# A fused attention and expert kernel on one core: one weight load, one table step, sixteen filler products and one cast are placed elsewhere

## The chip, the cores and the metric

The kernel runs on one core of a Trainium2 chip. A core has a matmul engine (TensorE, PE in the profile, with its weight loads as PEld), three engines for elementwise work (VectorE or DVE, ScalarE or ACT, GpSimd or POOL), and SyncE (SP), which here only issues transfers. Each engine works through its own list of instructions in order and waits on semaphores for the others. Transfers between the device memory and the on-chip memory (SBUF) run on 16 DMA engines; they are issued from SP, from ACT or from POOL. Matmul results are written to PSUM, from where DVE or ACT must read them.

The metric is the time of one execution on the device in microseconds (us).

## The reference

Two steps follow each other. The first is attention over 8 batches of 8 heads, 576 positions and 64 values per head, where a position sees only positions of its own block of 64 and of earlier blocks:

```python
scores = scale * np.matmul(q, k.transpose(0, 1, 3, 2))
mask = block_i >= block_j                       # blocks of 64 positions
scores = np.where(mask, scores, -1000000000.0)
attn = softmax(scores)
x = np.matmul(attn, v)                          # then (8, 576, 512): heads side by side
```

The second sends every position through one of eight experts, and an expert may be carried over from the position before:

```python
logits = np.einsum('bsd,de->bse', x, w_gate)
local_gate = sigmoid(x @ w_local)
fresh_e = int(np.argmax(logits[b, s]))
e = fresh_e if s == 0 or local_gate[b, s] < 0.5 else prev_e
out[b, s] = softmax(logits[b, s])[e] * (np.maximum(x[b, s] @ w1[e], 0.0) @ w2[e])
```

All inputs and the output are float32. w1 is 8 x 512 x 1024 and w2 is 8 x 1024 x 512.

## The kernel before

**Attention.** A loop over `it` from -2 to 31 handles one pair of heads per round, as a pipeline: in one round the pair `a = it + 2` is turned (queries and keys are transposed on PE), the pair `c = it + 1` gets its scores, the pair `e = it` is multiplied with v, and the pair `x = it - 1` is normalised and written out as bf16 rows to a table `x_rows` in device memory. The order of the work is written by hand (`tc.manual_schedule`): each engine gets its instructions in the order in which the Python code emits them. SP issues the loads of q, k and v (`load_qk`, `load_ends`, `load_v`) and the stores of x (`rows_x`). In between POOL issues the loads of the expert weights, which are cast to bf16 on the way: `weights(n)` takes the next n of 64 portions ("quarters", one row block of a w1 or w2), and `load_weights`, line 63, issues them. All weights stay in two large tiles, `w1_bf` and `w2_bf`. The last two portions belong to w2 of the eighth expert; their place in `w2_bf` holds small tables of the routing until shortly before.

**Routing.** While attention runs, DVE works out which expert each position takes, in four groups of two batches: `gate`, `fresh`, `scan_rows`, `chosen`, `ranks`. From this come tables of which rows of `x_rows` belong to which tile of 128 positions of one expert (`toka` for the tiles whose positions are known after two groups, `tokb` after three, `tok2g` and `tok2s` after all), and the expert of each tile (`tea`, `teb`, `te2`). A dictionary `plan`, filled with `at(it, where, f)`, says in which round and at which place of the round each of these steps is emitted.

**Experts.** The last part is a loop over tiles `t`. For a tile, `gather(t)` (line 763, POOL) fetches 128 rows of `x_rows` by an indirect DMA; `turn_rows(t)` (line 784, SP) transposes them by a DMA; `first(t)` (line 779, DVE) copies the expert's w1 out of `w1_bf` into one of two fixed places, which the trace calls `natb` and `plb`; `up(t)` (line 798, PE, with the Relu on ACT at line 802) is the first product; `down(t)` (line 813, PE) is the second one, read straight from `w2_bf` at an offset known only at run time, so it has to wait for all loads into `w2_bf`; ACT scales its result (line 816) and POOL writes it out with `scatter` (line 822). PE's order around the start is `up(0)`, `up(1)`, the transposes of the last pair of heads (`results`, lines 673 and 679), `down(0)`, `up(2)`, the gate sums (`sums`, line 732), `down(1)`, `up(3)`, `down(2)`, `up(4)` and so on. Two dictionaries, `ahead` and `steps`, hang the remaining routing steps on these tiles: in every round first the entries of `ahead`, then those of `steps`. For `t = 1`, `ahead` holds `sums`: the gate sums of the last heads on PE, their addition and transposition on DVE (lines 744 and 749). `steps` holds `whole_b(NTB)`, `shares_a(2)` and `shares(2)`: eleven short DVE instructions of the tables (lines 328 to 334 and 280 to 287) that use nothing of those sums. After them `first(4)` stands in DVE's list.

**The start.** `load_qk(0)` loads the first pair in six transfers, over SP and ACT. Until they land, `warm(26)` gives PE 26 products of a tile of ones with itself (line 837), into a PSUM tile that is not read. `turns()` for the first pair transposes the keys (`w = 1`), then the queries (`w = 0`), four products each (line 974); `turned` then copies keys on ACT and queries on DVE, the latter as two casts of 256 columns (line 846). `tails()` transposes the last 64 positions (line 1013), and the products for the row maxima begin with `top(0, 2)` (line 558).

Of the kernel before, what the change touches and what calls it, by code (L numbers as in the profile page):

```python
# [16 lines left out]
def kernel(  # L17
# [11 lines left out]
    nc = tc.nc  # L29
# [107 lines left out]
    XGB, XBB = 3, 2  # L137
# [284 lines left out]
    def g_tile(n):  # L422
        return ps_gp.tile([P, 512], F32, tag=f"g{n}", name=f"g{n}")
# [3 lines left out]
    with tc.manual_schedule():  # L427
# [9 lines left out]
        def const(shape, dt, name):  # L437
            return cst.tile(shape, dt, tag=name, name=name)
# [11 lines left out]
        qh = const([P, S + 192], BF16, "qh")  # L450
# [132 lines left out]
        def rows(h):  # L583
            return slice(64 * h, 64 * h + 64)
# [169 lines left out]
        def table(t):  # L754
            return ((toka, toka, tea, t) if t < NTA else
                    (tokb, tokb, teb, t - NTA) if t < NT1 else (tok2g, tok2s, te2, t - NT1))

        def gather(t):
            g = table(t)
            n = 2 * GC * P if t < NTA else 3 * GC * P if t < NT1 else BS  # L760
            z = t % (2 * XGB)
            xg = ffn["xg", t] = scr[:, z * XW:z * XW + XW] if z < XGB else xgs[z - XGB]
            nc.gpsimd.indirect_dma_start(
                out=xg, out_offset=None, in_=x_dram[0:n],
                in_offset=bass.IndirectOffsetOnAxis(ap=g[0][:, g[3]:g[3] + 1], axis=0),
                bounds_check=n - 1, oob_is_err=False)
# [68 lines left out]
        def warm(n):  # L835
            for _ in range(n):
                nc.tensor.matmul(warm_ps[:, 0:P], lhsT=ones, rhs=ones, start=True, stop=True)

        def turned(i, w, ps):

            if w:
                nc.scalar.copy(kh[:, 0:512], ps)
                nc.scalar.copy(pls[i][:, S:S + 512], ps)
                return
            for c in (0, 256):
                nc.vector.tensor_copy(qh[:, c:c + 256], ps[:, c:c + 256])

        def turned_rest(i, ps):
            nc.scalar.copy(pls[i][:, 0:512], ps)
# [3 lines left out]
        nc.scalar.copy(share[:, 0:1], ones[:, 0:1])  # L853
        load_qk(1)
        load_ends(1)
        warm(26)

        def scr_f(a, n):
            return scr[:, a:a + 2 * n].bitcast(F32)
# [15 lines left out]
        def at(it, where, f):  # L875
            plan.setdefault((it, where), []).append(f)
# [48 lines left out]
        at(30, "mid", lambda ps: slots(inva, toka, None))  # L925
        for t in range(XGB):
            at(30, "turn" if t > 1 else "begin", lambda ps, t=t: gather(t))
        at(30, "turn", lambda ps: weights(2))

        def run(it, where, ps=None):  # L930
            for f in plan.get((it, where), []):
# [5 lines left out]
        for it in range(-2, NPR):  # L937
            a, c, e, x = it + 2, it + 1, it, it - 1
# [16 lines left out]
            def weights(n):  # L955
                while n:
                    m = 2 if n > 1 and quarters[0] % 2 == 0 else 1
                    load_weights(quarters[0], m)
                    del quarters[:m]
                    n -= m  # L960
# [7 lines left out]
            def turns():  # L968

                pw[:] = g_tile(0), g_tile(1)  # L970
                if a == 0:
                    for w in (1, 0):
                        for t in range(4):
                            nc.tensor.transpose(pw[w][:, 128 * t:128 * t + 128],
                                                nat[:, 4 * w + t].rearrange("p h d -> p (h d)"),
                                                id_f)
                        turned(0, w, pw[w])
                    return
                for b in range(8):
                    turn_pair(b)  # L980
# [13 lines left out]
            def tails():  # L994

                tail = nat[:, 8].rearrange("p h d -> p (h d)") if on_a else None
                if on_x:
                    if it < NPR - 1:
                        g0, g1 = gx = g_tile(0), g_tile(1)
                    else:  # L1000
                        ps = seg_tile()
                        gx = ps[:, 0, :], ps[:, 1, :]
                        g1 = gx[1]
                    for m in range(5):
                        halves_x(x, gx, m)
                    if on_a:
                        for w, (g, c) in enumerate(((g0, 320), (g1, 384))):
                            nc.tensor.transpose(g[:, c:c + 64], tail[rows(w)],
                                                id_f[rows(w), rows(w)])
                else:  # L1010
                    g1 = g_tile(1)
                    if on_a:
                        nc.tensor.transpose(g1[:, 384:512], tail, id_f)
                run(it, "turned", g1)
                if on_a:
                    gq, gk, cq, ck = (g0, g1, 320, 384) if on_x else (g1, g1, 384, 448)
                    nc.scalar.copy(pl[:, 2 * S - 64:2 * S + 64].rearrange("p (a t) -> p a t", a=2),
                                   gk[:, None, ck:ck + 64].to_broadcast([P, 2, 64]))
                if on_x:
                    keep_halves(x, gx[1], 1)  # L1020
                    keep_ends(x, gx[1], 1)
                if on_a:
                    nc.scalar.copy(pl[:, 512:576], gq[:, cq:cq + 64])
                if on_x:
                    keep_halves(x, gx[0], 0)
                    keep_ends(x, gx[0], 0)
                if a == 0:
                    turned_rest(a, pw[0])
                return g1

            def tails_in():
                nc.gpsimd.tensor_copy(kh[:, 512:576], pl[:, 2 * S - 64:2 * S])
                nc.gpsimd.tensor_copy(qh[:, 512:576], pl[:, 512:576])
                q9 = qh.rearrange("p (b t) -> p b t", t=64)[:, 9:12:2, :]
                if a:
                    nc.gpsimd.tensor_copy(
                        q9, pl[:, 0:1024].rearrange("p (a t) -> p a t", a=2)[:, :, 0:64])
                else:
                    nc.gpsimd.tensor_copy(qh[:, 576:640], qh[:, 0:64])
                    nc.gpsimd.tensor_copy(qh[:, 704:768], qh[:, 512:576])  # L1040
# [6 lines left out]
            if it == -2:  # L1047
                turns()
                g1 = tails()
                tails_in()  # L1050
                load_qk(2)
                load_ends(2)
                top(0, 2)
                low_exchange(0)
                weights(2)
                mid_maxima(0)
                low_shift(0)
                opened = seg_tile()
                products(0, opened, 0, 0)
                products(0, opened, 0, 1)  # L1060
                high_maxima(0)
                continue
# [176 lines left out]
        def highb():  # L1239
# [4 lines left out]
        ahead = {0: [results],  # L1244
                 1: [sums],
                 6: [lambda: new_g(0, lambda ps: inverse(ps, ohl2, rhsb, nb, NTB))],
                 7: [lambda: new_g(1, lambda ps: rows_ps(ps, buf))],
                 14: [lambda: new_g(0, lambda ps: inverse(ps, ohl2, rhs2, NC_, NT2, range(n2)))],
                 15: [lambda: inverse(cur[2], ohl2, rhs2, NC_, NT2, range(n2, NC_))]}
        steps = {0: [lambda: whole(True)],  # L1250
                 1: [lambda: whole_b(NTB), lambda: shares_a(2), lambda: shares(2)],
                 2: [lambda: taken(t1k2[:, 0:nb], hi2[:, 0:nb], nb, tmp2[:, :, 0:nb])],
                 3: [lambda: taken_b(t1k2[:, 0:nb], hi2[:, 0:nb], nb),
                     lambda: tile_experts(teb, tend, NTB, tmpt2[:, 0:NTB, :])],
                 4: [lambda: shares_b(2), lambda: low2(0)],
                 5: [lambda: shares_out(2), highb, lambda: gate(last), lambda: fresh(last)],
                 6: [lambda: inverse_in(cur[2], invb, NTB), lambda: slots(invb, tokb, None),
                     lambda: fresh_b(last)],
# [22 lines left out]
        for t in range(NTM):  # L1281
            for z in (3, 4, 5) if t == 0 else wait_for.get(t, (t + 5,)):
                if z < NTM + 2:
                    gather(z)
            if t + 1 < NTM:
                ffn["woff", t] = offset(t, mybir.EngineType.PE)
                up(t + 1)
            if t + 2 < NTM + 2:
                turn_rows(t + 2)
            if t == 1:  # L1290
                cast_x(x, nc.gpsimd.tensor_copy)
            if t == 3:
                rows_x(x)
            for f in ahead.get(t, []) + steps.get(t, []):
                f()
            if t + 2 < NTM + 2:
                share_of(t + 2)
            down(t)
            for f in behind.get(t, []):
                f()  # L1300
            if t + 3 < NTM + 2:
                first(t + 3)
# [57 lines left out]
```

## Time and profile before

| what | value |
|---|---|
| three runs | 458.36, 458.43 and 460.65 us, median 458.43 us |
| the profiled execution | 454.2 us |
| its span, first to last instruction | 452.4 us |
| busy PE / DVE / ACT / POOL | 432.8 / 315.1 / 273.6 / 288.5 us |
| mean granted clock of PE | 0.995 |

The span is what the profiler records on the engines; the profiled execution's own time has 1.8 us around it. The profiled execution took 4.2 us less than the median of the three runs, so a sum built from the profile is first a difference, and is then put on the median.

The page of a profile gives the busy time of each engine, the span in 40 slices (here 11.3 us each), the queues of the transfers, and the chain of work that ended last. Beside it, the trace can be asked for a timeline: one row for instructions of one form that follow each other, with start, length, engine, line of the kernel, operation, what is written from what, and in square brackets how long the engine stood idle before it and who, by the semaphores, ended that. A view of windows gives each engine's busy time, the granted clock of PE and the load of the DMA engines in chosen stretches.

### The profile page before, as it was taken

The numbers are of one execution on the slowest core, as the hardware profiler recorded it, in microseconds if no ns is written. First come the engines' busy times: TensorE is split into PE (matmuls) and PEld (weight loads), VectorE is DVE, ScalarE is ACT, GpSimd is POOL, SyncE is SP. The second block draws the span as 40 slices with busy tenths as digits, with TensorE's granted clock in tenths as the row PEclk, the third lists the DMA queues.
The fourth block names the chain that finished last, engine by engine and source line by source line (L and its number), as shares of the span: only waits on it lengthen the run. The fifth ranks groups of instructions, "written<-read, shape, count | busy, mean of one in ns | idle before, by whom it ended". The sixth has DMA issues, their size and how long they took to land.

```text
span 452.4 us, 19648 instructions
## 1 busy us (share of the span) xinstructions
PE 432.8 (96%) x7738; PEld 338.2 (75%) x7738; DVE 315.1 (70%) x856; ACT 273.6 (60%) x573; POOL 288.5 (64%) x674
## 2 busy tenths in 40 slices
PE   7899999999999999999999999987999999999994
PEld 5688787787788877787878777776676777777772
DVE  4777667768778888887788897954876884333422
ACT  3857766766667657665766666554454555555552
POOL 4556566667566747675556665672777758878853
PEclk8999999999999999999999999999999999999999
DMA  8999699999999975999779898887655665546532
GB/s 152 190 164 188 143 173 164 195 186 171 185 181 175 186 162 117 203 161 183 158 143 184 149 179 152 146 139 104 146 137 153 137 147 149 151 130 167 141 116 80
DMA packets 169885, 71.15 MB, mean 157 GB/s; under 512 B 151424, under 2 KB 158080, under 8 KB 169792
## 3 DMA queue, kind: packets, MB, share of 16 engines
q1 hardware_dynamic: 154640, 38.05, 44.5%
q0 software_dynamic: 13952, 31.52, 34.4%
q8 instruction: 64, 1.05, 1.0%
q10 hardware_dynamic: 1200, 0.30, 0.3%
q14 instruction: 29, 0.24, 0.2%
HBM read 67.18 MB, written 14.97 MB: 182 GB/s over the span
## 4 chain that ended last, share of the span: by engine, by line
PE 41%; DVE 26%; POOL 12%; issue 11%; DMA 5%; ACT 2%; POOLq 1%; DVEq 0%; ACTq 0%
PE g L667 10%; DVE mx L577 9%; PE ps_s L625 8%; POOL out_dram L822 6%; PE ps_s L634 4%; PE ps_h L798 4%; DMA out_dram<-o_sb,tok2s 3%; PE g L659 3%; PE ps_m L558 3%; PE ps_o L813 3%; PE g L951 2%; PE g L732 2%; DVE diag L599 2%; POOL diag L599 1%; DMA x_rows<-w_bf 1%
## 5 line engine op out<-in xcount | busy, mean ns | idle before, releaser
L641 ACT ACTIVATE prob<-ps_s 128x640 f32<-128x640 f32 (+2 forms) x128 | 103.6, 839 | 41.3 <-PE ps_s L634 40.4
L577 DVE TENSOR_REDUCE mx<-ps_m 128x2 f32<-128x640 f32 (+2 forms) x96 | 100.2, 1044 | 26.9 <-PE ps_m L558 19.9
L625 PE MATMUL ps_s<-plb 64*128 64x320 f32 (+4 forms) x768 | 107.3, 400 | 0.7 <-DVE mx L579 0.7
L625 PEld LDWEIGHTS ps_s<-plb 64*128 64x128 f32 x768 | 68.0, 189 | 20.8 <-issue 9.8
L667 PE MATMUL g<-vt,prob 128*64 128x65 f32 x2560 | 80.3, 222 | 0.0
L667 PEld LDWEIGHTS g<-vt,prob 128*64 128x64 f32 x2560 | 77.5, 138 | 0.1
L813 PE MATMUL ps_o<-w_bf,hT 128*128 x304 | 71.5, 380 | 0.0
L802 ACT ACTIVATE hT<-ps_h 128x512 bf16<-128x512 f32 x76 | 45.4, 597 | 26.6 <-PE ps_h L798 26.2
L816 ACT ACTIVATE o_sb<-ps_o,share 128x512 f32<-128x512 f32 x37 | 25.4, 686 | 40.2 <-PE ps_o L813 35.7
L813 PEld LDWEIGHTS <-hT 128*128 128x128 bf16 x304 | 28.0, 98 | 27.8 <-issue 0.3
L590 POOL COPY mx<-mx 64x2 f32<-64x2 f32 x64 | 11.7, 183 | 52.3 <-DVE mx L581 49.7
L779 DVE COPY natb<-w_bf 128x4096 bf16 x20 | 24.7, 1235 | 27.5 <-PE ps_h L798 25.2
L779 DVE COPY plb<-w_bf 128x4096 bf16 x20 | 25.1, 1253 | 24.6 <-PE ps_h L798 24.1
L798 PEld LDWEIGHTS <-plb 128*128 128x128 bf16 x608 | 35.4, 98 | 6.8 <-issue 2.9
L798 PEld LDWEIGHTS <-natb 128*128 128x128 bf16 x608 | 35.4, 98 | 6.2 <-DVE rs L541 1.5
L558 PE MATMUL ps_m<-kh,qh 64*128 64x320 bf16 (+3 forms) x256 | 37.6, 324 | 2.5 <-DVE mx L581 1.4
L634 PE MATMUL ps_s<-diag,ones 64*128 64x448 bf16 (+1 forms) x372 | 36.8, 274 | 2.0 <-DVE diag L599 0.4
L822 POOL DMA_INDIRECT out_dram<-o_sb,tok2s x17 | 28.7, 1690 | 11.6 <-ACT o_sb L816 7.0
L63 POOL DMA_DIRECT2D w_bf<-in_moe_w_dram x56 | 33.4, 596 | 1.4 <-DMA x_rows<-xb 0.4
L987 ACT COPY plb<-g 128x512 f32<-128x512 f32 x62 | 33.2, 593 | 0.3 <-PE g L951 0.2
L651 POOL MEMSET prob<- 64x128 f32 x128 | 24.5, 206 | 11.1 <-ACT prob L641 5.0
L798 PE MATMUL ps_h<-scr,plb 128*128 128x128 bf16 x416 | 25.3, 219 | 2.6 <-DVE share L788 2.3
(285 smaller groups left out, 769.8 us busy)
## 6 DMA issues: line engine op xcount, KB each, us to landing
w_bf<-in_moe_w_dram POOLq DMA_DIRECT2D x48, 256.0 KB, 4.5
vt<-in_v_dram SPq DMA_DIRECT2D x64, 128.0 KB
natb<-in_k_dram SPq DMA_DIRECT2D x63, 128.0 KB
natb<-in_q_dram SPq DMA_DIRECT2D x63, 128.0 KB
w_bf<-in_moe_w_dram POOLq DMA_DIRECT2D x8, 512.0 KB, 5.5
x_rows<-w_bf SPq DMA_DIRECT2D x13, 256.0 KB
natb<-in_k_dram SPq DMA_DIRECT2D x32, 32.0 KB
vt<-in_v_dram SPq DMA_DIRECT2D x32, 32.0 KB
```

Of the source, the lines that this page charges most:

```text
L63: nc.gpsimd.dma_start(out=dst[:, e * WE:(e + 1) * WE].rearrange("p (k f) -> p k f", k=n)[:, r:r + m, :], in_=view[e][:, r:r + m, :])
L558: nc.tensor.matmul(ps[:, h, c:c + w], lhsT=qh[rows(h), 64 * b:64 * b + 128], rhs=kh[rows(h), 0:w], start=True, stop=m is None)
L577: nc.vector.reduce_max(mx[:, b:b + 2], ps[:, :, 0:w], axis=AX)
L625: nc.tensor.matmul(ps[:, h, c:c + n], lhsT=pls[i][rows(h), S + 128 * j:S + 128 * j + 128], rhs=pls[i][rows(h), a:a + n], start=part == 0, ...
L634: nc.tensor.matmul(ps[:, h, c:c + n], lhsT=ones[rows(h), :], rhs=diag[rows(h), a // 64:(a + n) // 64, :], start=False, stop=part == len(SE ...
L641: nc.scalar.activation(p[:, :, SEG0[s]:SEG0[s] + w], ps[:, :, 0:w], func=AF.Exp, scale=scale_attn)
L667: nc.tensor.matmul(g[rows(e), o + 65 * h:o + 65 * h + 65], lhsT=p[:, h, c:c + 64], rhs=t[:, j, h, :], start=(j == 0), stop=(j == m))
L779: nc.vector.tensor_copy(w, w1_bf[:, bass.ds(off, WE)])
L798: nc.tensor.matmul(ps_h[:, f, :], lhsT=w[:, f0 + ko * F:f0 + ko * F + 2 * P - 1:2], rhs=xb[:, ko * P:(ko + 1) * P], start=(ko == 0), stop= ...
L802: nc.scalar.activation(hT[:, half * 4:half * 4 + 4, :], ps_h, func=AF.Relu)
L813: nc.tensor.matmul(ps_o, lhsT=hT[:, fo, :], rhs=w2_bf[:, bass.ds(woff + fo * Dm, Dm)], start=(fo == 0), stop=(fo == FO - 1))
L822: wr = nc.gpsimd.indirect_dma_start(out=out_flat, out_offset=bass.IndirectOffsetOnAxis(ap=g[1][:, g[3]:g[3] + 1], axis=0), in_=o_sb, in_of ...
```

## The change

Four things are placed differently; no arithmetic of the result changes.

1. **The last two weight portions.** `weights(2)` leaves round 30, where it stood behind the gather of tile 2, and is emitted in the expert part, for `t = 0`, behind the gather of tile 3 (`XGB` is 3) and ahead of those of tiles 4 and 5.
2. **The tables of `t = 1`.** For that tile alone `steps` comes before `ahead`: the eleven table instructions stand ahead of the addition of the gate sums in DVE's list.
3. **Products of ones.** 29 instead of 26 at the start, 5 between the transposes of the first keys and of the first queries, and 8 behind `tails()` of the first pair.
4. **The first queries' cast.** Columns 0 to 255 stay on DVE; columns 256 to 511 go to ACT.

```diff
-            for c in (0, 256):
-                nc.vector.tensor_copy(qh[:, c:c + 256], ps[:, c:c + 256])
+            nc.vector.tensor_copy(qh[:, 0:256], ps[:, 0:256])
+            nc.scalar.copy(qh[:, 256:512], ps[:, 256:512])
...
-        warm(26)
+        warm(29)
...
-        at(30, "turn", lambda ps: weights(2))
...
                         turned(0, w, pw[w])
+                        warm(5 * w)
                     return
...
                 g1 = tails()
+                warm(8)
                 tails_in()
...
             for z in (3, 4, 5) if t == 0 else wait_for.get(t, (t + 5,)):
                 if z < NTM + 2:
                     gather(z)
+                if z == XGB:
+                    weights(2)
...
-            for f in ahead.get(t, []) + steps.get(t, []):
+            for f in steps.get(t, []) + ahead.get(t, []) if t == 1 else ahead.get(t, []) + steps.get(t, []):
                 f()
```

## The prediction

> **What bounds the kernel now.** I read the page first: where PE is busy, and how loaded the transfers are.
>
> ```profile
> PE   7899999999999999999999999987999999999994
> ...
> PEclk8999999999999999999999999999999999999999
> ...
> DMA  8999699999999975999779898887655665546532
> ...
> w_bf<-in_moe_w_dram POOLq DMA_DIRECT2D x8, 512.0 KB, 5.5
> ```
>
> PE is the bound nearly everywhere. Three places are weak: the first slice (with a lower clock), and slices 27 and 28, from 294 to 317 us, where attention hands over to the experts. All parts of the change lie in these places. The last line is the price of a weight load of the size that is moved: 5.5 us from issue to landing, as a median.
>
> The second view is the timeline of the hand-over, PE first, then POOL and SP, whose lists hold the moved load and the transfers beside it.
>
> ```profile
> 301.86 1.80 PE L667 MATMUL g<-vt,prob 128*64 128x65 f32 x56
> 305.08 1.95 PE L798 MATMUL ps_h<-scr,natb 128*128 128x128 bf16 x32 [1.42 <-DMA scr<-scr]
> 309.30 1.95 PE L798 MATMUL ps_h<-scr,plb 128*128 128x128 bf16 x32 [2.27 <-DVE share L788]
> 311.08 0.61 PE L673 MATMUL g<-id_f,x 128*128 128x128 f32 x4
> ...
> 311.89 1.90 PE L813 MATMUL ps_o<-w_bf,hT 128*128 x8
> ...
> 322.06 1.95 PE L798 MATMUL ps_h<-scr,natb 128*128 128x128 bf16 x32 [0.46 <-DVE tmp L302]
> ```
>
> ```profile
> 297.97 1.03 POOL L763 DMA_INDIRECT scr<-x_rows,toka  x1 [0.24 <-issue]
> 299.00 0.79 POOL L63 DMA_DIRECT2D w_bf<-in_moe_w_dram  x1
> 300.97 0.91 POOL L651 MEMSET prob<- 64x128 f32 x1 [1.18 <-ACT prob L641]
> 302.04 1.86 POOL L763 DMA_INDIRECT xg<-x_rows,toka  x1 [0.16 <-issue]
> 304.21 1.01 POOL L763 DMA_INDIRECT xg<-x_rows,toka  x1 [0.30 <-issue]
> 305.52 1.00 POOL L763 DMA_INDIRECT xg<-x_rows,toka  x1 [0.30 <-issue]
> 314.79 1.04 POOL L822 DMA_INDIRECT out_dram<-o_sb,toka  x1 [8.27 <-ACT o_sb L816]
> ```
>
> ```profile
> 298.37 3.18 SPq L784 DMA_TRANSPOSE scr<-scr  x2
> ...
> 302.67 0.39 SPq L518 DMA_DIRECT2D x_rows<-qh  x1
> ...
> 303.83 4.72 SPq L784 DMA_TRANSPOSE xb<-scr  x1
> ```
>
> PE ends attention at 303.66, does `up(0)` at 305.08, then stands until `up(1)` at 309.30, and `down(0)` starts at 311.89. `up(0)` waits for the transposed rows of tile 0. For `up(1)` the row names a DVE step (line 788) that computes no input of it; its inputs are a copy of w1 that DVE ended at 302.97 (next fence) and the transposed rows of tile 1. So I take it that `up(1)` too waits for its transpose, issued from 298.37 to 301.55. The moved load of 512 KB was issued at 299.00, into the middle of these.
>
> ```profile
> 301.66 1.31 DVE L779 COPY plb<-w_bf 128x4096 bf16 x1
> ...
> 307.29 1.23 DVE L779 COPY natb<-w_bf 128x4096 bf16 x1 [0.31 <-PE ps_h L798]
> ...
> 316.30 0.52 DVE L744 TENSOR_TENSOR lgS<-g,lgS 128x128 f32<-128x128 f32 x2 [3.79 <-PE g L732]
> ...
> 317.40 0.51 DVE L328 TENSOR_TENSOR_SCAN sm<-ones,sm 128x8 f32<-128x8 bf16 x1
> ...
> 319.76 0.17 DVE L287 TENSOR_TENSOR pgs<-sm 128x9 f32<-128x9 f32 x1
> ...
> 320.25 1.23 DVE L779 COPY natb<-w_bf 128x4096 bf16 x1 [0.26 <-issue]
> ```
>
> ```profile
> 300.00:302.00 2.00, 2.00 (x64) 1.87 (x62) 1.49 (x2) 1.95 (x8) 0.91 (x1) 1.00 0.92 113
> 302.00:304.00 2.00, 1.66 (x58) 1.52 (x54) 1.90 (x6) 0.64 (x2) 1.86 (x1) 1.00 1.07 173
> 304.00:306.00 2.00, 0.92 (x17) 0.95 (x18) 1.79 (x10) 0.00 (x0) 1.49 (x2) 1.00 1.14 110
> 306.00:308.00 2.00, 1.03 (x19) 0.91 (x17) 1.59 (x7) 1.19 (x2) 0.52 (x1) 1.00 1.60 61
> ```
>
> These windows end with PE's clock, the load of the DMA engines and GB/s. The engines are full, at 306 to 308 fuller than full, yet move only 61 GB/s: transposes and weights are in each other's way.
>
> **Part 1, the weight load.** *What goes at 299.00.* POOL gains nothing by it: behind it stands a fill that waits for ACT until 300.97 anyway, so the gather at 302.04 stays. The transposes of tiles 0 and 1 get the DMA engines without the load. A later one bounds their price alone:
>
> ```profile
> 435.69 1.19 SPq L784 DMA_TRANSPOSE scr<-scr  x1
> ...
> 439.38 1.84 PE L798 MATMUL ps_h<-scr,natb 128*128 128x128 bf16 x30
> ```
>
> From issue to the product that reads it are 3.7 us at most. The second transpose has started its issue by 301.55 - 1.19 = 300.36, so it lands by about 304.1. Then `up(0)` starts when PE is free, about 303.7, `up(1)` 1.8 us later (the pitch is 311.08 - 309.30), ending at 307.3, and `results` takes 311.89 - 311.08 = 0.8: PE is ready for `down(0)` at 308.1 instead of 311.89. The result of the last heads that `results` reads is then due 3.8 us earlier than before; DVE does not idle before 307, so I allow 0.3 of delay there, hidden in the wait that follows.
>
> *What comes at 303.9.* The load goes behind the gather that ends at 302.04 + 1.86 = 303.90. It delays POOL's next two gathers by 0.8 us; behind them POOL idled 8.27 us, and their rows are needed by `up(4)` and `up(5)` only, so that is hidden. (Were it not, it would cost 0.8.) The gather of tile 3 now runs ahead of the load on POOL's queue. New is that `down(0)` waits for this landing, and behind `down(0)` stands everything that PE has left. The landing is the unknown. Low end: the median of 5.5, so 309.4. High end: how far gathers in this very stretch were held up by the same crowd.
>
> ```profile
> xg<-x_rows,toka POOLq DMA_INDIRECT x3, 6.3
> ...
> DMA to landing us min/median/max: 2.8/3.2/6.3
> ```
>
> The three gathers issued from 302.04 to 305.52 took 6.3 us as a median, where the median of all gathers is 3.2: 3.1 us more. Added to 5.5 that gives 8.6, landing at 312.5. The new stretch has the transpose of tile 2 (303.83), the x rows (302.67) and three gathers in it, but not tiles 0 and 1, so it is neither calm nor as full; I take the middle, 7.05, landing at 310.95. `down(0)` then starts 0.94 us before 311.89. Bounds: 2.49 earlier (309.4) to 0.61 later (312.5).
>
> **Part 2, the tables.** Before, DVE idled 3.79 us until the sums' matmuls at 316.30, added and transposed them until 317.40, then did eleven short steps until 319.93, then `first(4)` at 320.25, and PE waited 0.46 us for it at 322.06. The eleven steps are 2.5 us (317.40 to 319.93) and fit the 3.79 us of idle time; `first(4)` comes 2.5 us earlier, so the 0.46 us on PE goes. Late next is nothing but PE itself, whose rows are closed around it. If PE comes to the sums a microsecond earlier, the cover still holds, since the `plb` copy before it moves up as well. Gain 0.46; bounds 0 (something else also ended at 322.06) and 0.46.
>
> **Parts 3 and 4, the start.**
>
> ```profile
> 6.00:7.00 1.00, 0.45 (x5) 0.15 (x3) 0.76 (x2) 0.20 (x2) 0.00 (x0) 1.00 1.31 196
> ...
> 8.00:9.00 1.00, 1.00 (x8) 0.56 (x8) 1.00 (x3) 0.00 (x0) 0.09 (x1) 0.50 0.59 134
> ...
> 6.18 0.76 DVE L846 CAST qh<-g 128x256 bf16<-128x256 f32 x2 [3.93 <-PE g L974]
> ...
> 9.69 0.28 DVE L581 TENSOR_REDUCE mx<-ps_m 128x2 f32<-128x128 f32 x1
> ...
> 10.71 1.23 DVE L577 TENSOR_REDUCE mx<-ps_m 128x2 f32<-128x1024 f32 x1 [0.74 <-PE ps_m L558]
> ...
> 48.52 0.72 POOL L505 CAST w_bf<-x 128x640 bf16<-128x640 f32 x1 [1.64 <-DMA x_rows<-w_bf]
> ```
>
> PE is under half busy at 6 to 7 us, and afterwards its clock is at half. Splitting the cast halves 0.76, so the queries come 0.38 us earlier, but eight products stand before their first reader. At half clock these and the split may lose some 0.4; if the clock stays full, DVE's reduction at 10.71 loses its wait of 0.74. None of it should reach the end: at 48.52 POOL waits 1.64 us for a store of x, which hangs on SP's transfers, not on PE. An earlier PE only waits longer there. I take 0, with ends -0.74 and +0.4.
>
> The Trainium skill, TensorE: Matmul & The Clock Gate (What's actually happening), says that a monitor grants the full clock after a busy window of some 3.4 us and takes it away after an idle one, and that the windows run freely. By that rule the products in the gaps would keep the clock, and the end of the sum would be -0.74 instead of 0, in some executions. The trace agrees so far as the half clock follows on the idle microsecond.
>
> **Sum.** -0.94 - 0.46 + 0 = -1.4 us: 452.8 on the profiled execution's 454.2, and 457.0 on the median of 458.43. PE is closed from here to the last tiles, so a shift of PE here reaches the end.
>
> **Rivals.**
>
> *The load lands in its plain 5.5 us* (faster). `down(0)` at 309.4 gives -2.49 - 0.46 = -2.95, so 455.5. For it: no large DVE copy runs from 302.97 to 307.29, behind the new issue, while one did behind the old one (301.66); with the clock kept, 454.7. Against it: the transpose of tile 2 is issued at the same moment. The Trainium skill, SBUF — State Buffer (SBUF: two separate sides), holds that DVE copies keep POOL from writing a transfer's descriptors; by it this rival wins. The trace shows a slow stretch behind such copies, but not the cause.
>
> *`down(0)` stands behind a late load* (slower). If the crowd stretches the load in proportion, 5.5 x 6.3 / 3.2 = 10.8 us, it lands at 314.7, `down(0)` is 2.8 later, and the time is 458.43 + 2.8 - 0.46 = 460.8. It loses from a landing at 312.35 on, and by more than the noise from 314.65 on. For it: POOL's place is later, the reader's is the same. Against it: two of the three transposes are gone by then.
>
> *`up(1)` waits for DVE after all*, as its row says. Then PE is not ready sooner, `down(0)` stays at 311.89 and only the tables gain: 458.0. Against it: line 788 feeds only ACT's scaling.
>
> **How the numbers follow.** This kernel's runs can't tell a change under about 0.5%, 2.3 us, from none. Chances: forecast 0.40 and the DVE rival 0.12, both within; plain landing 0.33, faster; late load 0.15, slower. The likeliest case's own range is 455.5 to 459.4 (the landing's ends and +0.4 from the start); the range over the cases, without the last part of the slow one, is 454.5 to 459.9.
>
> **What would show it.** `up(1)` right behind `up(0)` and both before 308; a row for `down(0)` with a wait on the weight transfer near 311; the table steps before line 744 and no wait at `up(4)`; full clock at 8 to 9 us, and at 48 us a longer wait of POOL for the same store. I am wrong if `up(1)` still stands at 309, if `down(0)` starts after 312.4, or if the start's gain passes 48 us.

## The result, and the profile after

The kernel before took 459.25 us (median of 19 runs), the changed one 462.45 us (19 runs): ratio 1.0056, 95% interval 1.0029 to 1.0083. Ratios, here and below, leave out runs that fell into a slower state of the chip, here three of the changed kernel's, and so are not quite the quotients of the medians (here 1.0070). The changed kernel is slower by about half a per cent, just over what this kernel's runs can tell from nothing; the forecast was 457.0 us. The profiled execution of the changed kernel took 462.88 us, its span is 461.2 us, 8.8 us more than the 452.4 us of before. But the profiled execution of before, 454.2 us, was faster than every one of its 19 runs (456.10 us the lowest), while that of the changed kernel lies near its median.

The page of the changed kernel, in 40 slices as before (one slice is now 11.5 us):

```profile
PE   8899899999899999999999999997999999999993
...
PEclk9999999999999999999999999999999999999999
DMA  7999699999999986998797898859556545555531
...
L813 PE MATMUL ps_o<-w_bf,hT 128*128 x304 | 71.7, 379 | 2.6 <-DMA w_bf<-in_moe_w_dram 2.4
```

The first slice has lost its low clock, one weak slice is left where there were two, and a new idle time has appeared: `down` (line 813) waits 2.4 us for the weights. The timeline of PE shows where:

```profile
306.77 1.80 PE L667 MATMUL g<-vt,prob 128*64 128x65 f32 x56
308.51 1.96 PE L798 MATMUL ps_h<-scr,natb 128*128 128x128 bf16 x32
310.30 1.95 PE L798 MATMUL ps_h<-scr,plb 128*128 128x128 bf16 x32
...
313.43 1.04 PE L813 MATMUL ps_o<-w_bf,hT 128*128 x4
316.91 1.02 PE L813 MATMUL ps_o<-w_bf,hT 128*128 x4 [2.44 <-DMA w_bf<-in_moe_w_dram]
317.88 1.95 PE L798 MATMUL ps_h<-xb,natb 128*128 128x128 bf16 x32
...
325.69 1.50 PE L798 MATMUL ps_h<-scr,natb 128*128 128x128 bf16 x24
```

The two waits of before, 1.42 and 2.27 us, are gone, and only the second half of `down(0)` waits for the load, because the two moved portions are the second half of w2 of the eighth expert, and a product whose expert is known only at run time waits for the rows of its place in every expert. POOL and the chain of waits give the load's landing:

```profile
306.82 1.80 POOL L763 DMA_INDIRECT xg<-x_rows,toka  x1 [0.16 <-issue]
308.61 0.79 POOL L63 DMA_DIRECT2D w_bf<-in_moe_w_dram  x1
```

```profile
308.61 8.25 DMA w_bf<-in_moe_w_dram
```

8.25 us from issue to landing. A yardstick for all that follows is the *hand-over*: from the end of attention (end of the last row of line 667) to the start of `up(4)`. Before it is 322.06 - 303.66 = 18.40 us, after 325.69 - 308.57 = 17.12 us. By this pair of executions the hand-over gained 1.28 us, close to the 1.40 us of the forecast, and the loss lies elsewhere: attention ends 4.91 us later, and the part behind `up(4)` takes 461.2 - 325.69 = 135.5 us instead of 452.4 - 322.06 = 130.3. The waits of PE's weight loads from 340 to 440 us show part of the latter, in total, times and longest (before, the same line had 0.5 us, once):

```profile
PEld L798 <- issue: 3.3, 8, 0.7
```

A comparison of the two traces thus says: hand-over right, 10 us lost where the change touches nothing. The experiments show that it is nearly the reverse.

### The profile page after: what moved, and what is told of

It is laid out like the page before. It is cut to its first block, busy times and chain, and to the rows that moved or that the text cites. A ratio compares the mean times of both kernels' runs of the same rounds, so it can differ in the third digit from the quotient of the medians.

```text
span 461.2 us, 19682 instructions
## 1 busy us (share of the span) xinstructions
PE 436.8 (95%) x7754; PEld 340.8 (74%) x7754; DVE 313.0 (68%) x855; ACT 272.0 (59%) x574; POOL 285.0 (62%) x674
## 4 chain that ended last, share of the span: by engine, by line
PE 49%; DVE 24%; DMA 9%; issue 7%; POOL 6%; ACT 2%; POOLq 1%; DVEq 0%; ACTq 0%
PE g L667 9%; DVE mx L577 9%; PE ps_h L798 8%; PE ps_o L813 8%; PE ps_s L625 7%; PE ps_s L634 4%; DMA out_dram<-o_sb,tok2s 4%; PE g L659 3%; PE ps_m L558 3%; DMA x_rows<-w_bf 3%; PE g L950 2%; PE g L732 2%; DMA w_bf<-in_moe_w_dram 2%; POOL out_dram L822 2%; DVE diag L599 2%
## 5 line engine op out<-in xcount | busy, mean ns | idle before, releaser
L802 ACT ACTIVATE hT<-ps_h 128x512 bf16<-128x512 f32 x76 | 44.1, 597 | 41.4 <-PE ps_h L798 32.0
L822 POOL DMA_INDIRECT out_dram<-o_sb,tok2s x17 | 22.1, 1301 | 17.6 <-ACT o_sb L816 14.0
L599 POOL TENSOR_TENSOR diag<-negi,mx 128x384 bf16<-128x384 f32 x31 | 25.6, 826 | 3.3 <-PE ps_s L634 0.6
```

The lines of the kernel that those rows point to most:

```text
L599: eng.tensor_tensor((diag1 if i else diag0)[:, b:b + n, :], negi[:, None, :].to_broadcast([P, n, 64]), mxs[i][:, z:z + n, None].to_broadca ...
L802: nc.scalar.activation(hT[:, half * 4:half * 4 + 4, :], ps_h, func=AF.Relu)
```

## The experiments

All ratios are to runs of the kernel before on the same chip in the same set.

| run | what it has | ratio (95% interval) |
|---|---|---|
| first set: before 460.72 us | | |
| e1_weights | part 1 | 1.0066 (1.0033 to 1.0100) |
| e2_start | parts 3, 4 | 1.0044 (1.0013 to 1.0075) |
| e4_no_products | parts 1, 2, 4 | 1.0006 (0.9976 to 1.0037) |
| e5_pad16 | before, 16 products between up(0) and up(1) | 1.0032 (1.0006 to 1.0058) |
| second set, another chip: before 455.84 us | | |
| e0_before | nothing | 0.9967 (0.9937 to 0.9997) |
| e3_tables | part 2 | 0.9965 (0.9930 to 0.9999) |
| e8_weights_tables | parts 1, 2 | 1.0045 (1.0006 to 1.0083) |
| e11_tables_cast | parts 2, 4 | 0.9977 (0.9944 to 1.0010) |
| third set, a third chip: before 455.20 us | | |
| e12_after | all | 1.0040 (1.0007 to 1.0074) |
| e13_ahead | parts 1, 2, load ahead of the gather | 0.9939 (0.9909 to 0.9969) |
| e14_fill | parts 1, 2, fill in down(0) | 0.9998 (0.9965 to 1.0032) |
| e15_start_tables | parts 2, 3, 4 | 0.9983 (0.9949 to 1.0017) |
| fourth and fifth set, a fourth chip: before 455.81 and 455.78 us | | |
| e16_gathers_later | parts 1, 2, gathers 4 and 5 later | 1.0058 (1.0027 to 1.0088) |
| e17_turn2_later | parts 1, 2, transpose of tile 2 later | 1.0026 (0.9988 to 1.0063) |
| e18_all_ahead | all, load ahead of the gather | 0.9977 (0.9948 to 1.0006) |
| e19_ahead_alone | part 1, load ahead of the gather | 0.9940 (0.9911 to 0.9969) |
| e20_ahead_same_chip | as e13 | 0.9927 (0.9891 to 0.9963) |
| e21_all_ahead_same_chip | as e18 | 0.9977 (0.9941 to 1.0013) |

The unchanged kernel as e0 came out at 0.9967, so a difference of 0.3% between two kernels is nothing, whatever its interval says.

### Which part loses: the parts alone

The theories at the start: the added products shift PE's instruction list (*list theory*); the earlier start shifts transfers in attention (*transfer theory*); the moved load itself costs (*load theory*). e1, e2 and e4 take the diff of the change apart: e1 has only the `weights(2)` lines, e2 only the two casts and the three `warm` lines, e4 leaves out the three `warm` lines. e5 adds to the kernel before:

```diff
         up(0)
+        for _ in range(16):
+            nc.tensor.matmul(ffn["ps_h"][2][:, 0, :], lhsT=ones, rhs=ones, start=True, stop=True)
         first(2)
```

> Only part 1: the last two weight portions move behind the gather of tile 3; start, tables and casts as before. Prediction on record for this part: -0.94 us (-2.49 to +0.61). List theory (the slowdown comes from the 32 PE instructions that the added products put ahead of everything else, so that PE's 16 KB instruction blocks end at other places): PE's list keeps its length here, so nothing is lost, -0.9 to -1.3 us, ratio 0.997 to 0.998. Transfer theory (the earlier start moves the stores of x against the loads, and attention loses): the start is as before, so also -0.9 to -1.3. Load theory (the moved load itself costs in the expert loop): +3 us or more, ratio above 1.005. Hand-over in the profile: from the end of attention to the start of up(4) 17.1 to 17.5 us instead of 18.4.

> Only parts 3 and 4: 29, 5 and 8 products and the split cast; weights and tables as before. Prediction on record: 0 us (-0.74 to +0.4). List theory: the expert loop shows PE stalls with no semaphore behind them (3 to 5 us in all between 340 and 440 us), and the whole is 4 to 6 us slower, ratio 1.009 to 1.013. Transfer theory: attention ends 3 to 5 us later and the expert loop keeps its pitch; ratio 1.006 to 1.010. Load theory: ratio 1.000, within 0.2%.

> Parts 1, 2 and 4 without part 3: no added products, so PE's list has its old length up to the expert part. List theory: the gain at the hand-over stays (-1.2 us), the stalls in the expert loop are gone: ratio 0.996 to 0.998, end about 1.2 to 1.7 us earlier than before. Transfer theory: the clock is at half again at 8 to 9 us, so the start is nearly that of before, and attention loses at most 1 us: ratio 0.996 to 1.000; the stalls in the expert loop are its weak point, as it has no reason for them to go. Load theory: ratio 1.005 or more, as after the whole change.

> The kernel before with 16 products of ones between up(0) and up(1), where PE stands 2.27 us: they take about 0.9 us of that gap, write what up(1) overwrites, and shift PE's list by 32 instructions for the expert part alone. List theory: attention as before, PE stalls without a semaphore in the expert loop as after the change (3 to 5 us): ratio 1.007 to 1.011. Transfer theory and load theory: no change, ratio 0.999 to 1.001, PE's waits for issue in 340 to 440 us 0.5 us as before.

Measured: e1 1.0066, the largest loss of the four, as the load theory had it. e1 also shows the stalls "of the expert loop", with PE's list as long as before:

```profile
PEld L798 <- issue: 4.1, 9, 1.1
```

So the list theory falls for them. e4, which also has the moved load, lost nothing that can be told from 0.3%, against the load theory; it came out 3.3 us under e1 (460.97 against 464.26), with a wait of 2.48 us for the load where e1 has 4.20 us. So the load does not cost the same in every kernel that has it. e2 ends attention at 305.04, not the 3 to 5 us later of the transfer theory, and its loss is left to the last set. e5, between the expectations, is no more than 0.3%. All four kernels of this set have 2.5 to 4.6 us in this row, and behind `up(4)` they take 133.6 to 137.2 us. The kernel before was slow on this chip too: 460.72 us, against 455.2 to 455.8 on the three others.

### The kernel before once more, the tables, and part 1 with them

e0 is the kernel before, unchanged; e3 has only part 2's line, e8 parts 1 and 2, e11 part 2 and the split cast.

> The kernel before once more, unchanged, to see a second execution of it by its profile. Luck theory (the profiled execution of before was a fast one, and the 2.27 us of wait at up(1) were its own): up(1) follows up(0) without a wait, up(4) waits for DVE's copy about 1.8 us instead of 0.46 us, from the end of attention to up(4) 17.2 to 17.6 us instead of 18.4, and the expert part behind up(4) takes 133 to 137 us instead of 130.3. Theory of the prediction: up(1) waits about 2 us again, 18.4 us, and 130 us behind. Ratio 1.000 in both, within 0.3%.

> Only part 2, the tables ahead of the sums' addition. Prediction on record: -0.46 us. Luck theory: the load stays at its old place and up(1) has no wait, so PE comes to up(4) earlier and DVE's copy for it is what is late; the tables ahead then gain about 1.8 us, ratio 0.995 to 0.997. By the order of the first set (weights alone +3.0 us, weights, tables and cast +0.3 us) the tables would be worth up to 2.7 us.

> Parts 1 and 2 without the start. Prediction on record: -1.4 us. Late-load theory (the moved load lands 8 to 9 us after its issue, the second half of down(0) stands 2.5 to 4 us for it and PE's clock falls to half behind it): from the end of attention to up(4) 17 to 20 us, ratio 0.999 to 1.004, 2 to 4 us slower than the tables alone.

> Parts 2 and 4: tables and the split cast, no products added, load at its old place. If the start costs by its products alone: as the tables alone, ratio 0.994 to 0.997. If the split cast costs (ACT gets work at the start, 2 us by the run of the start alone): 1.8 us above the tables alone, ratio 0.999 to 1.001.

The hand-over of e0 on PE:

```profile
306.93 2.53 PE L798 MATMUL ps_h<-scr,natb 128*128 128x128 bf16 x32 [2.17 <-DMA scr<-scr]
309.25 3.04 PE L798 MATMUL ps_h<-scr,plb 128*128 128x128 bf16 x32
...
312.93 1.90 PE L813 MATMUL ps_o<-w_bf,hT 128*128 x8
...
323.12 1.95 PE L798 MATMUL ps_h<-scr,natb 128*128 128x128 bf16 x32 [0.48 <-DVE tmp L302]
```

Attention ends here at 304.76, so the hand-over is 18.36 us, as in the first execution, and behind `up(4)` lie 453.1 - 323.12 = 130.0 us. The sums speak against the luck theory, the rows only in part: `up(1)` follows `up(0)` without a wait, as that theory had it. The time goes into one wait of 2.17 us and into PE's clock, which fell behind it (0.55 from 308 to 309 us, 0.50 from 309 to 311), so that `up(0)` and `up(1)` take 2.53 and 3.04 us instead of 1.95. And in e2, whose load also stands at its old place, PE's rows are these:

```profile
305.04 1.95 PE L798 MATMUL ps_h<-scr,natb 128*128 128x128 bf16 x32
306.82 0.67 PE L798 MATMUL ps_h<-scr,plb 128*128 128x128 bf16 x9
...
310.98 1.90 PE L813 MATMUL ps_o<-w_bf,hT 128*128 x7
...
322.29 1.95 PE L798 MATMUL ps_h<-scr,natb 128*128 128x128 bf16 x32 [1.59 <-DVE tmp L302]
```

`up(0)` and `up(1)` start without a wait (`up(1)` then pauses three times, 1.1 us in all), `down(0)` comes 5.9 us behind the end of attention (305.04), and then `up(4)` waits 1.59 us for DVE. With the load at its old place, `down(0)` started 8.23, 8.17, 8.97, 5.37, 5.94, 6.12 and 5.84 us behind attention (before, e0, e3, e11, e2, e5 with its 16 products, e15). Without any wait it starts 310.00 - 305.68 = 4.3 us behind attention (e8, below). So the 3.8 us that the prediction took away were there in full in three of seven executions, and the other four had 1.1 to 1.8 us of them. In e0 and e3 they were one wait at `up(0)` (2.17 and 2.96 us) and a slow clock behind it; a wait of 2.27 us at `up(1)` is in the first profile alone.

The tables alone gave 0.9965 against 0.9967 for the unchanged kernel: nothing that the time shows, although the wait at `up(4)` is gone. e3 on PE:

```profile
304.00 1.80 PE L667 MATMUL g<-vt,prob 128*64 128x65 f32 x56
308.77 2.92 PE L798 MATMUL ps_h<-scr,natb 128*128 128x128 bf16 x32 [2.96 <-DVE ints L271]
...
314.77 1.90 PE L813 MATMUL ps_o<-w_bf,hT 128*128 x8
...
324.32 1.95 PE L798 MATMUL ps_h<-scr,natb 128*128 128x128 bf16 x32
```

Its hand-over is 324.32 - 305.80 = 18.5 us. Part 1 on top of the tables (e8, 458.39 us against 454.88) cost 3.5 us. e8 on PE, then its windows (PE's clock stands before the load of the DMA engines and GB/s), then its chain:

```profile
305.62 1.96 PE L798 MATMUL ps_h<-scr,natb 128*128 128x128 bf16 x32
...
310.00 1.04 PE L813 MATMUL ps_o<-w_bf,hT 128*128 x4
315.64 1.87 PE L813 MATMUL ps_o<-w_bf,hT 128*128 x4 [4.60 <-DMA w_bf<-in_moe_w_dram]
317.30 3.62 PE L798 MATMUL ps_h<-xb,natb 128*128 128x128 bf16 x32
...
326.79 1.95 PE L798 MATMUL ps_h<-scr,natb 128*128 128x128 bf16 x32
```

```profile
310.00:312.00 2.00, 1.04 (x8) 0.41 (x5) 1.65 (x7) 0.59 (x2) 0.00 (x0) 1.00 1.04 34
...
314.00:316.00 2.00, 0.35 (x1) 0.10 (x1) 0.73 (x4) 0.00 (x0) 0.00 (x0) 0.50 0.97 249
...
318.00:320.00 2.00, 2.00 (x22) 2.00 (x20) 0.00 (x0) 0.83 (x2) 1.18 (x2) 0.50 0.02 2
```

```profile
305.85 9.75 DMA w_bf<-in_moe_w_dram
```

The load lands 9.75 us after its issue, PE stands 4.60 us, and then works at half clock: `up(2)` takes 3.62 us instead of 1.95. The hand-over is 326.79 - 305.68 = 21.1 us. In the changed kernel's first profile the same wait was 2.44 us and the clock stayed at full, and so that execution did not show the loss.

### The place of the load, and the clock behind the wait

e12 is the whole change again, e15 the change without part 1. e13 and e14 start from e8:

```diff
# e13
             for z in (3, 4, 5) if t == 0 else wait_for.get(t, (t + 5,)):
+                if z == XGB:
+                    weights(2)
                 if z < NTM + 2:
                     gather(z)
-                if z == XGB:
-                    weights(2)
# e14, in down(t)
                                  start=(fo == 0), stop=(fo == FO - 1))
+                if t == 0 and fo == FO // 2 - 1:
+                    for _ in range(48):
+                        nc.tensor.matmul(ffn["ps_h"][1][:, 0, :], lhsT=ones, rhs=ones,
+                                         start=True, stop=True)
```

> The whole change again, beside the kernel before on the same chip. Recorded ratio 1.0056. Two explanations of the PE stalls between 374 and 440 us: if the added products make them (they shift PE's list), they are here again on any chip, 3 to 5 us; if they belong to the chip of the first set, where four kernels all showed them and none of the four of the second set but one, they come or go with the other three kernels of this set. Ratio by the first 1.008 to 1.012 on a chip without stalls of its own, by the second 1.003 to 1.008. Hand-over: landing 8 to 10 us after the load's issue.

> Parts 1 and 2 with the load ahead of the gather of tile 3 instead of behind it, about 2 us earlier on POOL's list. If the landing follows the issue (8 to 9.7 us behind it), it comes 2 us earlier, the wait in down(0) is 2 to 2.6 us instead of 4.6, PE keeps most of its clock, and it is 2 to 3 us faster than the load behind the gather: ratio 0.998 to 1.001. If the transposes of tiles 2 and 3 hold the load whenever it is issued, the landing stays and the ratio is 1.004 to 1.008.

> Parts 1 and 2 with 48 products of ones (about 2.7 us at full clock) between the two halves of down(0), where PE waits 4.6 us for the load; they write what up(2) overwrites. Clock theory (of the 3.3 us that the moved load costs about 0.9 is its later landing, and 2.5 the half clock behind PE's idle time, seen in up(2) of 3.56 us instead of 1.95): the clock stays at full, up(2) takes 1.95 us, from the end of attention to up(4) 18.3 to 19 us instead of 21.1, ratio 0.998 to 1.002. If the landing alone costs, nothing changes: 1.0045 to 1.008.

> Parts 2, 3 and 4: the start with its products and the split cast, and the tables; the load at its old place. If the start costs about 2 us, as the run of the start alone had it: ratio 1.000 to 1.004. If that was chance, and the start costs nothing: as the tables alone, 0.995 to 0.999.

e12 repeats the result, 1.0040, and ends the matter of the stalls: with the added products in place, PE's weight loads of line 798 wait from 340 to 440 us

```profile
PEld L798 <- issue: 0.8, 2, 0.6
```

and behind `up(4)` it takes 454.7 - 324.23 = 130.5 us, as before; attention ends at 305.06, not 308.57. Its loss sits at the hand-over, 19.17 us: the load lands after 8.90 us, PE waits 3.48 us, and `up(2)` runs partly at half clock.

```profile
313.90 1.02 PE L813 MATMUL ps_o<-w_bf,hT 128*128 x4 [3.48 <-DMA w_bf<-in_moe_w_dram]
314.84 3.24 PE L798 MATMUL ps_h<-xb,natb 128*128 128x128 bf16 x32
```

Against e15, the same kernel without part 1 on the same chip, the medians differ by 457.14 - 454.49 = 2.65 us. e14, with the fill:

```profile
310.38 2.84 PE L818 MATMUL ps_h<-ones 128*128 128x128 bf16 x48
313.06 1.03 PE L813 MATMUL ps_o<-w_bf,hT 128*128 x4
313.92 1.95 PE L798 MATMUL ps_h<-xb,natb 128*128 128x128 bf16 x32
...
321.73 1.95 PE L798 MATMUL ps_h<-scr,natb 128*128 128x128 bf16 x32
```

From the second half of `down(0)` to `up(4)` are 8.67 us, where e8 took 326.79 - 315.64 = 11.15: 2.5 us for the half clock alone. The ratio falls from 1.0045 to 0.9998. In this execution the load was there when the fill ended, 7.7 us after its issue at 305.35 or sooner, so a part of the gain in its profile is an earlier landing; the clock is what the fill is meant for and what the rows show.

e13 is the fastest of its set, 0.9939, faster than both of its expectations. POOL and PE:

```profile
302.42 1.28 POOL L63 DMA_DIRECT2D w_bf<-in_moe_w_dram  x1
304.00 1.07 POOL L763 DMA_INDIRECT xg<-x_rows,toka  x1 [0.31 <-issue]
```

```profile
308.57 1.04 PE L813 MATMUL ps_o<-w_bf,hT 128*128 x4
309.77 1.02 PE L813 MATMUL ps_o<-w_bf,hT 128*128 x4 [0.15 <-DMA w_bf<-in_moe_w_dram]
311.40 1.95 PE L798 MATMUL ps_h<-xb,natb 128*128 128x128 bf16 x32 [0.61 <-DVE sm L328]
...
319.21 1.95 PE L798 MATMUL ps_h<-scr,natb 128*128 128x128 bf16 x32
```

The gather that stands ahead in the change takes POOL 1.8 us; without it in front the load is issued about 2 us sooner, lands at most 309.77 - 302.42 = 7.35 us later, and PE waits 0.15 us. Attention ends at 304.25, so the hand-over is 15.0 us. What is late next is `up(2)`. That row alone would prove little, as e11 and e15, with the load at its old place, have hand-overs of 14.9 and 15.4 us too; the gain is in the medians, on this chip 452.19 us against 454.49 for e15 and 455.20 for the kernel before.

### What stretches the landing, and what the start costs

e16 and e17 start from e8, e19 is e1 with e13's swap, e18 and e21 are the whole change with it, e20 is e13.

```diff
# e16
-            for z in (3, 4, 5) if t == 0 else wait_for.get(t, (t + 5,)):
+            for z in (3,) if t == 0 else (4, 5, 6) if t == 1 else wait_for.get(t, (t + 5,)):
# e17
-            if t + 2 < NTM + 2:
-                turn_rows(t + 2)
+            for z in {0: (3, 2), 1: ()}.get(t, (t + 2,)):
+                if z < NTM + 2:
+                    turn_rows(z)
```

> Parts 1 and 2, with the gathers of tiles 4 and 5 behind the first result's store instead of behind the load. If these gathers stretch the load, it lands 6 to 7.3 us after its issue instead of 9.75. If the transposed rows of tile 2, issued beside it, stretch it, it lands at 8 to 10 us as before. Tiles 4 and 5 come later in this kernel, so up(4) may wait and its time is no measure of the load.

> Parts 1 and 2, with the transpose of tile 2 behind that of tile 3 on SP's list, so that it waits for the gather of tile 3 and is no longer issued beside the load. If the transpose stretches the load, it lands 6 to 7.3 us after its issue and PE's wait in down(0) is 1 to 2.5 us. If it is the gathers, 8 to 10 us. up(2) comes later in any case, so the whole may be slower.

> The whole change with one swap: the load ahead of the gather of tile 3 instead of behind it. The place of the load being the only harm, it is as fast as parts 1 and 2 with that swap: ratio 0.991 to 0.997. If the products and the split cast cost of themselves, 0.997 to 1.001.

> Part 1 alone with the load ahead of the gather of tile 3, tables as before. With tables it was 0.9939. If the tables are worth 1.8 us once PE comes early (up(4) waits for DVE's copy as in the run of the start alone, where up(3) to up(4) took 5.27 instead of 3.51 us), the ratio is 0.996 to 1.000 and that row shows the wait; if they are worth nothing, 0.992 to 0.996.

> Parts 1 and 2 with the load ahead of the gather of tile 3, now on the same chip as the next run. If the gain is the kernel's and not the chip's: ratio 0.992 to 0.996.

> The same with parts 3 and 4. If the start costs nothing, within 0.2% of the run before; if it costs what the two chips suggested, 0.3 to 0.5% (1.4 to 2.3 us) slower than it, with attention ending later by as much.

e16, without the gathers of tiles 4 and 5 beside it: issue at 305.97, the waiting product starts at 314.29, 8.3 us. The gathers of tiles 4 and 5 are not what stretches the load; that of tile 3, still ahead of it, was not tried by itself. e17, with the transpose of tile 2 out of its way: 306.97 to 314.55, 7.6 us, the shortest of those with a wait at this place (8.2 to 9.8 in after, e1, e4, e8, e12 and e16), but still over the 7.3 at which I would have called the transpose the cause. PE's wait, 2.39 us, is within what the transpose would give. But in e14 the transpose was issued beside the load too (305.34 and 305.35), and the load was there after 7.7 us or sooner. So the transpose may be a part of it; that stays open. Where the traces give a landing for the load ahead of the gather of tile 3, it is 7.3 us in e13 and 6.6 in e20, and at its old place 6.6, 7.3 and 7.2 us (e0, e3, e15).

e19 shows that the swap alone carries the gain, 0.9940 without the tables, and e20 repeats e13 with 0.9927. The tables' 1.8 us were not found there either, as another wait set the pace: in e18, e19 and e21 `up(2)` waited 1.7 to 2.1 us for its transposed rows, and in e19, behind 2.09 us, it ran at half clock (3.47 us). In e20's profile, with 457.3 us the slowest of its 13 runs, it waited 2.80 us and lost the clock as well (the row names a DVE step whose result `up(2)` does not read):

```profile
314.28 3.50 PE L798 MATMUL ps_h<-xb,natb 128*128 128x128 bf16 x32 [2.80 <-DVE pgs L287]
```

The start seems to cost: on the same chip 454.96 (e21) against 452.68 us (e20), 2.3 us, and resampling the runs of both gives 0.7 to 3.1 us for the difference of their means. e2 alone had 1.0044. Against it, e15 came out at 0.9983, in the range for a start that costs nothing, and e12 (1.0040) is no slower than e8 (1.0045). Where it would be lost I can't say: POOL waits longer for the store of x in most profiles with the start (next section), and attention ends at 306.17 in e21 against 305.13 in e20, but at 304.54 in e18, the same kernel as e21.

## Why the prediction was wrong

The forecast was 457.0 us in a range of 454.5 to 459.9, with 0.15 for slower. It was slower. (The ends of the range follow from no sum that the prediction shows; the nearest are 454.7 and 459.4.) Its steps in order:

**Part 1, what goes at 299.00: right for that execution, wrong as a price.** `up(1)` follows `up(0)`, and `down(0)` begins 4.9 us behind attention (313.43 - 308.57) instead of 8.2: 3.4 us earlier, where 3.8 was forecast. The rival that `up(1)` waits for DVE is out: with the load gone it waited for nothing in after, e1, e4, e8 and e12, and in e0 it ran at 309.25, ahead of the DVE step of line 788 that the first profile names (311.33). But 3.8 us that three of seven executions have in full are worth less than 3.8 us, and e0 and e3 had them by a wait of `up(0)` and the clock, not by one of `up(1)`.

**Part 1, the landing: the step that failed.** The prediction put it 7.05 us after the issue, at most 8.6. In the six executions named above it was 8.2 to 9.8, beyond the upper bound in three. The step took the middle because tiles 0 and 1 were out of the way; the transpose of tile 2 is issued at the very moment of the load (305.85 in e8), and the DMA engines were full at 34 GB/s from 310 to 312. From the end of attention, the second half of `down(0)` starts in e8 315.64 - 305.68 = 9.96 us later; in e0 it was some 9.1 (312.93 + 0.95 - 304.76) and in e3 some 9.9: 0 to 0.9 us of loss in place of 0.94 of gain. It would have been worse had the whole of `down(0)` waited, as the prediction had it; the first half runs ahead, which is worth 0.95 us.

**Part 1, the term left out: the clock.** No bound of the sum held what a long wait does to PE behind it. 2.5 us in e8 (11.15 - 8.67). Together 2.5 to 3.4 us, where the profiles of e8 and e3 differ by 21.1 - 18.5 = 2.6 us at the hand-over and the medians by 3.5 (e8 and e3) and 2.65 us (e12 and e15). It is no fixed price: the profile of the changed kernel kept its clock, and e4's median lies only 0.25 us above the kernel before. So that these two terms also make up the 3.2 us of the result is inferred from the later runs and not seen in its profile. The slower rival had the right mechanism, the late load; its landing of 10.8 us was too late, and it too left the clock out, so that its 2.3 us of loss come near the 2.55 us of e8 over the kernel before by luck. It belonged ahead of the plain landing of 5.5 us, which none of the seven waits at this place showed. The Trainium skill, SBUF — State Buffer (SBUF: two separate sides), by whose rule the plain landing was to win, is neither borne out nor refuted. The rival's condition was met, as no copy of line 779 ran from the load's issue to 312.01 in after (issue at 308.61) and to 309.25 in e8 (305.85), and the landing was late all the same: what made it late was something else than these copies.

The Trainium skill, TensorE: Matmul & The Clock Gate (What's actually happening), gives a free-running window of about 3.4 us of idle time after which the clock falls to half. The waits of 4.60 us (e8) and 4.20 us (e1), after which the clock was at 0.50, agree; of two waits of nearly one length, 2.44 us in after and 2.48 us in e4, the first kept the clock and the second did not, which a free-running window allows. That waits of 2.48 us (e4), 2.17 us (e0) and 2.09 us (e19, at 0.50 from 313 to 314 us) were enough at all is shorter than the page's window of idle time, and here the measurement decides.

**Part 2: the mechanism held, the size can't be seen.** The tables stand ahead, in the changed kernel's DVE rows:

```profile
315.40 0.17 DVE L328 TENSOR_TENSOR_SCAN sm<-ones,sm 128x8 f32<-128x8 bf16 x1
...
317.41 0.17 DVE L287 TENSOR_TENSOR pgs<-sm 128x9 f32<-128x9 f32 x1
...
321.93 0.52 DVE L744 TENSOR_TENSOR lgS<-g,lgS 128x128 f32<-128x128 f32 x2 [4.35 <-PE g L732]
```

No wait is left at `up(4)`. Without part 2 the wait was 0.46 and 0.48 us (before, e0) where `down(0)` came late and 1.59 and 1.58 us (e2, e5) where it came early; the medians of e3 and e0 differ by nothing.

**Parts 3 and 4: the clock is kept, the gain is eaten, and more.** The windows of the changed kernel and POOL's wait, which in before was 2.3 us in total, twice, with a longest of 1.6:

```profile
8.00:9.00 1.00, 0.76 (x9) 0.52 (x9) 1.00 (x2) 0.06 (x1) 0.37 (x3) 1.00 0.53 120
```

```profile
POOL w_bf L505 <- DMA x_rows<-w_bf: 6.3, 4, 3.4
```

Full clock at 8 to 9 us, where it was 0.50, and a longer wait of POOL for the store of x: both as written. "None of it should reach the end" held for the gain, as far as e2 (1.0044) and e15 (0.9983, against 0.9965 for the tables alone) can tell; a cost of 2.3 us, as between e21 and e20, would be outside its ends of -0.74 and +0.4, and whether it is there, and why, is open.

**The base.** The 10 us that the two traces show in attention and behind `up(4)` are not the change's: e12 has neither. A part of them is that the first trace took less time than any of the 19 runs. The stalls behind `up(4)` seem to come with a chip, as all four kernels of the first set had them and of the other 14 only e11; which chip the two first profiles come from is not on record. I read them first as an effect of the added products; the runs took that away.

## What to carry to other kernels

A wait that one profiled execution shows is a sample: profile the unchanged kernel a second time before taking the wait's length for a gain. A load moved closer to its reader needs a landing bounded by the most crowded stretch of the trace and, if PE may stand for it, a term for the clock behind the wait. Where a transfer and its neighbours on one queue differ in urgency, the order between them is worth trying first: here one swap with a gather that was needed later turned +0.45% into -0.6% (e13; -0.7% in e20) for parts 1 and 2, which beats both kernels.

## What was not expected of the hardware

- A wait of PE can cost more than its own length: 2.5 us were lost at half clock behind 4.60 us of idle time (e8), and even around a wait of 2.48 us (e4, until 313.08) the clock was 0.60 from 312 to 314 us and 0.55 from 314 to 316; 2.09 us were enough in e19. 48 products of ones in the gap, 2.84 us, kept it at full.
- One load of 512 KB took at most 7.35 us when issued 2 us ahead of a transpose (302.42, the transpose of tile 2 at 304.42, e13) and 9.75 us when issued with it (both 305.85, e8). One such pair is no rule: in e14, issued with it as well, it took at most 7.7 us.
- Chips, or the times at which they ran, differ for this kernel: 460.7 us on one, 455.2 to 455.8 on three, with PE waiting 2.5 to 4.6 us on nothing that the profile names (340 to 440 us) in all four kernels on the one. On the other three 13 of 14 kernels had at most 1.6 us there; e11 had 3.3.
